# One product of 104 columns for y and the state in a chunked RWKV-7 kernel with a hard-swish feed-forward

## The chip, the cores and the metric

The kernel runs on one core of one Trainium2 chip. The metric is the device time of one execution in microseconds (us), as the median of several runs. Its engines are TensorE (PE; its weight loads are listed as PEld), VectorE (DVE), ScalarE (ACT), GpSimd (POOL) and SyncE, whose queue (SPq) issues nearly all DMAs.

## What is computed

Four sequences of 768 tokens, 8 heads of 40 features. A state of 40 x 40 per head is carried over the tokens; then comes a feed-forward with a hard-swish.

```python
for t in range(S):
    y[:, :, t] = np.einsum('bhd,bhde->bhe', rt, state)
    Sa = np.einsum('bhde,bhe->bhd', state, at)
    state_decay = state * wt[:, :, None, :] - np.einsum('bhd,bhe->bhde', Sa, bt)
    state = state_decay + np.einsum('bhd,bhe->bhde', vt, kt)
...
h = x @ w_in                       # x: y as (3072, 320); w_in: 320 x 2048
g = h * np.clip(h + 3.0, 0.0, 6.0) / 6.0
out = g @ w_out                    # w_out: 2048 x 320
```

All is fp32.

## The kernel before

**Units.** The recurrence is done in blocks of 64 tokens. A unit is such a block for two sequences, so a tile of 128 partitions holds 2 x 64 tokens (or 2 x 64 slots of features, 40 of them used). There are 24 units in 6 groups of 4. Unit i continues the state tile `state[i % 2]`.

**Stages ahead of the state** (`prepare`), which do not depend on it: W and gam (decays, by two scans on VectorE, lines 555 and 566), A, B and K (transposed a, b and k times decays), F (products of a and b; four units' F together are inverted by many small steps on VectorE and GpSimd, `invert`, into `tinv`), factor (decays turned, then k and b times them into `KBt`), E (masked scores of k and a) and EV (scores times v, line 701).

**Stages on the state** (`step`): RT and VT (turned r and v; the state is scaled by the decay, line 855), R and S (from the state), U and UT (by `tinv`, lines 906 and 926), rS (the part of y from the old state), C and H (scores, masked into one of three score buffers by `masked`, line 530; the scores' products are at line 522), sn (the new state: KBt's columns as weights, v and U as moving data, line 961; added at line 969), y (the same columns as weights, the masked scores as moving data, line 984; added at line 995 and multiplied by the decays on GpSimd at line 996), move and move2 (DMAs that bring y into the layout of the feed-forward, lines 1010 and 1015).

Most of these products are 64 x 64 or smaller and run as four independent ones on the quarters of the PE array. Each fp32 product leaves two records in the profile.

**Feed-forward** (`feed_forward`): products `h` (line 1066), relu and hard-swish into `gt` on ScalarE (1081) and VectorE (1082), products `o` (1107). `pieces` issues this work in small pieces between the blocks of the recurrence; two banks of `h` alternate, so the next products into a bank wait until its gt is done.

**Order.** All instructions are in a hand-written order on each engine's queue. From unit 4 on the loop goes by blocks, four to a unit. In each block `together` first issues the products of all stages that are due, by PRODUCTS, and then what follows them on the other engines, by RESULTS. It may use five PSUM banks at a time; where a stage would need more, it finishes what it has begun first. `ps_pair` places products of up to 512 columns in a pair of banks. Between blocks come pieces of feed-forward and steps of the inversion. In the steady state (units 8 and later) the stages of the current unit and those of the unit five ahead share the blocks:

| block | current unit | unit before | units ahead |
|---|---|---|---|
| 0 | RT, VT | y | W, gam; EV of the one before it |
| 1 | R, C, S | move, move2 | A, B |
| 2 | U, UT, rS | | F, K |
| 3 | sn, H | | E, factor |

Units 8 to 11 are prepared at a closer distance with CLOSE_STAGES.

Of the kernel before, what the change touches and what calls it, by code (L numbers as in the profile page):

```python
# [17 lines left out]
P = 128  # L18
# [13 lines left out]
def kernel(  # L32
# [178 lines left out]
    wms = [const.tile([P, SCAN + 1], F32, name=f"wm{i}") for i in range(2)]  # L211
    for t in wms:
        nc.vector.memset(t[:], 0.0)
# [6 lines left out]

    score = []
    for i in range(3):
        t = const.tile([P, H, BL], F32, name=f"score{i}")
        nc.gpsimd.memset(t[:], 0.0)
        score.append(t)
    turn = [0]

    values = [padded(const.tile([P, H, SLOT], F32, name=f"V{i}"), f"V{i}") for i in range(AHEAD)]
# [283 lines left out]
    def half(i, n=SLOT):  # L512
        return slice(SLOT * i, SLOT * i + n)

    def scores(lhs, rhs, swap=False):


        o = ps_pair(NPR, BL)
        for n in range(NPR):
            for q in range(2):  # L520
                for i in range(2):
                    nc.tensor.matmul(out=o[i][half(q), n, :],  # L522
                                     lhsT=lhs[half(i, D), n ^ (2 * q * swap), half(q)],
                                     rhs=rhs[half(i, D), n, half(q)], start=True, stop=True)
        return o

    def masked(o):
        turn[0] += 1
        x = score[turn[0] % len(score)]
        nc.vector.copy_predicated(out=x[:].rearrange("p (i h) t -> p i h t", i=2), mask=mask8, data=o[2])  # L530
        return x


    def prepare(i, F):
        n, o = i % NU, data[i]
        halves = i >= 2 * NU
        def w_stage():
            wt = turn_pairs(o["WN"])
            yield PE

            wm = o["wm"] = wms[i % 2]
# [12 lines left out]
            prods = o["prods"] = tmp.tile([P, NB, 2, HB + 1], F32, name="prods", bufs=2)  # L554
            nc.vector.tensor_tensor_scan(  # L555
                out=prods[:].rearrange("p r m i -> p (r m i)"), data0=wm[:, 0:SCAN], data1=start[:],
                initial=0.0, op0=ALU.mult, op1=ALU.add,
            )

        def gam_stage():  # L560

            prods, wm = o["prods"], o["wm"]
            first = start[:].rearrange("p (n i) -> p n i", i=HB + 1)[:, :, 0]
            nc.vector.reciprocal(first, prods[:].rearrange("p r m i -> p (r m) i")[:, ::-1, HB])
            back = _ap(wm[:], SCAN, [[-1, SCAN]])
            nc.vector.tensor_tensor_scan(out=back, data0=back, data1=start[:], initial=0.0,  # L566
                                         op0=ALU.mult, op1=ALU.add)
# [12 lines left out]

            copy(gv[:, :, 0:HB], _ap(o["wm"][:], HB + 1, [[row, NB], [-1, HB]]))
            copy(rv[:, :, HB:BL], _ap(o["wm"][:], HB + 3, [[row, NB], [1, HB]]))
            nc.gpsimd.tensor_copy(gv[:, :, HB:BL], o["prods"][:, :, 1, 0:HB])  # L583
            nc.gpsimd.tensor_copy(rv[:, :, 0:HB], o["prods"][:, :, 0, 0:HB][:, :, ::-1])
            dec = grp.tile([P, 2, 2, NPR], F32, name="dec", tag="dec", bufs=NU + 2)
            nc.gpsimd.tensor_copy(dec[:].rearrange("p m q r -> p r q m"),
                                  o["prods"][:].rearrange("p (r q) m i -> p r q m i", q=2)[:, :, :, :, HB])
            o["dec"] = dec
            if NU + 1 < i <= 2 * NU:
                fetch("V", i)  # L590
            yield from ()

        def a_stage():
            x = turn_in(o["AN"], halves)
            yield PE
            nc.vector.memset(_ap(o["wm"][:], 0, [[HB + 1, 2 * NB + 1]]), 0.0)
# [92 lines left out]
        def e_stage():  # L689
            x = scores(o["kt"], o["at"])  # L690
            yield PE
            o["E"] = masked(x)

        def ev_stage():

# [136 lines left out]
    def step(i):  # L832
# [52 lines left out]
        def s_S():  # L885
# [10 lines left out]
            new_U()  # L896
# [16 lines left out]
        def s_C():  # L913
            x = scores(m["VT"], m["RT"])
            yield PE
            m["K"] = masked(x)

        def s_UT():

            up = ps_pair(2, P)  # L920
# [11 lines left out]
            nc.scalar.activation(out=m["UT"][:].rearrange("p (x j) t -> p x j t", x=2), in_=up[2],  # L932
                                 func=AF.Copy, scale=-1.0)

        def s_rS():

# [12 lines left out]
                                 in_=ysp[2].rearrange("p r j q t -> p r j (q t)"), func=AF.Copy)  # L949

        def s_sn():
            wide = SLOT if i < NU else D
            sn = ps_pair(NPR, D)
            for name in "KB":
                for pr in range(NPR):
                    for s in range(2):
                        for q in range(2):
                            h = 2 * pr + s
                            by = VN[half(q), 4 * s + pr, 0:D] if name == "K" else \
                                m["U"][half(q), 4 * (s ^ q) + pr, 0:D]  # L960
                            nc.tensor.matmul(  # L961
                                out=sn[q][half(s, wide), pr, :],
                                lhsT=o[name][half(q), h * D:h * D + wide], rhs=by,
                                start=(name == "K" and pr == 0), stop=(name == "B" and pr == NPR - 1),
                            )
            yield PE
            for rows in [slice(0, P)] if i < NU else [half(s, D) for s in range(2)]:
                x = st[rows, :, :, 0:D]
                nc.vector.tensor_tensor(out=x, in0=sn[2][rows], in1=x, op=ALU.add)  # L969

        def s_H():
            x = scores(m["UT"], m["RT"], swap=True)
            yield PE
            m["B"] = masked(x)

        def s_y():
            y = ps_pair(NPR, BL)
# [35 lines left out]
        def s_move2():  # L1013
            for dst, src in m["moves"][4:]:
# [3 lines left out]

        return {"RT": s_RT, "R": s_R, "VT": s_VT, "S": s_S, "U": s_U, "C": s_C, "UT": s_UT,
                "rS": s_rS,  # L1020
                "sn": s_sn, "H": s_H, "y": s_y, "move": s_move, "move2": s_move2}

# [313 lines left out]
    for _ in range(18):  # L1336
# [149 lines left out]
```

## Time and profile before

| | |
|---|---|
| median of the runs shown | 788.37 us (788.35, 788.37, 791.86) |
| the profiled execution | 791.42 us, its span 789.7 us |
| mean granted TensorE clock | 0.963 |
| PE busy | 729.7 us (92%), 15832 instructions |
| DVE, ACT, POOL busy | 496.0, 320.6, 174.7 us |

The span is from the first to the last instruction. Busy times of PE overlap where products follow each other, since their ends are modelled; distances from start to start do not. Lines are those of the kernel before. A row of groups or of the timeline gives the line, the engine, the operation, the tiles written and read, and the shapes; in the timeline it begins with start and duration in us.

### The profile page before, as it was taken

What the parts mean: (1) busy time and instruction counts of PE and PEld (TensorE: products, weight loads), DVE (VectorE), ACT (ScalarE), POOL (GpSimd) and SP (SyncE); (2) the same over time, 40 slices, a digit from 0 to 9 for tenths busy, and PEclk for the clock granted to TensorE, in tenths of its full rate; (3) what the DMA queues carried; (4) which work ended last, traced back from release to release, by engine and by line L of the source; (5) the groups of instructions that cost most, each with busy time, mean ns of one, the idle gap of its engine ahead of it and who ended that gap; (6) DMA issues with size and microseconds to landing.
All of it is one profiled execution on the core that took longest, in us unless ns stands there. A gap on an engine that the chain in (4) does not pass through costs nothing.

```text
span 789.7 us, 35306 instructions
## 1 busy us (share of the span) xinstructions
PE 729.7 (92%) x15832; PEld 619.4 (78%) x15832; DVE 496.0 (63%) x971; ACT 320.6 (41%) x664; POOL 174.7 (22%) x318
## 2 busy tenths in 40 slices
PE   5726888999999989999999999999999999999998
PEld 4625777778778778888888888888888888888886
DVE  7899867699545699345988445987435982323210
ACT  2376865324445334444334444335434225412211
POOL 6403111322232304112404212304312202000000
PEclk9865699999999999999999999999999999999999
DMA  9684453311333313223213223213221101110000
GB/s 122 114 201 123 109 165 70 70 27 36 56 62 60 64 28 57 50 44 67 44 29 64 45 46 63 48 28 65 45 51 38 31 10 30 30 30 10 13 20 17
DMA packets 174215, 45.03 MB, mean 57 GB/s; under 512 B 157424, under 2 KB 172784, under 8 KB 174064
## 3 DMA queue, kind: packets, MB, share of 16 engines
q1 hardware_dynamic: 169760, 42.03, 27.5%
q8 instruction: 125, 2.05, 1.0%
q10 hardware_dynamic: 4304, 0.74, 0.7%
q14 instruction: 26, 0.21, 0.1%
HBM read 34.08 MB, written 3.93 MB: 48 GB/s over the span
## 4 chain that ended last, share of the span: by engine, by line
PE 80%; DVE 8%; DMA 4%; issue 3%; ACT 2%; SPq 2%; POOL 0%; DVEq 0%
PE h L1066 27%; PE o L1107 24%; PE pair L522 4%; PE pair L984 3%; PE one L484 2%; PE pair L494 2%; PE pair L961 2%; PE pair L906 2%; PE pair L868 1%; PE pair L926 1%; PE pair L942 1%; SPq L468 1%; PE pair L811 1%; PE pair L701 1%; DVE wm L566 1%
## 5 line engine op out<-in xcount | busy, mean ns | idle before, releaser
L1066 PE MATMUL h<-xt,win 128*128 128x128 f32 (+1 forms) x2304 | 249.0, 282 | 3.3 <-DVE gt L1082 3.3
L1066 PEld LDWEIGHTS h<-xt,win 128*128 128x128 f32 (+1 forms) x2304 | 229.6, 191 | 20.3 <-issue 4.2
L1107 PE MATMUL o<-wout,gt 128*128 128x320 f32 x768 | 229.6, 442 | 0.0
L1107 PEld LDWEIGHTS o<-wout,gt 128*128 128x128 f32 x768 | 138.1, 190 | 50.2
L1082 DVE SCALAR_TENSOR_TENSOR gt<-gt,h 128x512 f32<-128x512 f32 x96 | 62.0, 681 | 74.4 <-ACT gt L1081 74.4
L1081 ACT ACTIVATE gt<-h,three 128x512 f32<-128x512 f32 x96 | 62.1, 686 | 96.0 <-PE h L1066 95.6
L996 POOL TENSOR_TENSOR yg<-ys,gam 128x512 f32<-128x512 f32 x22 | 39.0, 1772 | 156.7 <-DVE ys L995 77.1
L753 DVE TENSOR_TENSOR prod<-x 128x30 f32<-128x30 f32 (+9 forms) x180 | 67.2, 373 | 8.9 <-POOL x L738 3.3
L674 POOL TENSOR_TENSOR KBt<-K,rgt 128x320 f32<-128x320 f32 x22 | 19.0, 865 | 217.8 <-ACT rgt L663 169.6
L759 DVE TENSOR_TENSOR x<-x,prod 128x30 f32<-128x30 f32 (+9 forms) x180 | 62.2, 346 | 5.5
L969 DVE TENSOR_TENSOR state<-pair,state 40x320 f32<-40x320 f32 (+1 forms) x43 | 21.0, 488 | 62.8 <-PE pair L961 36.5
L530 DVE COPY_PREDICATED score<-mask,pair 128x512 f32<-128x512 int32 x72 | 50.6, 722 | 1.5 <-PE pair L522 1.0
L995 DVE TENSOR_TENSOR ys<-pair,ys 128x512 f32<-128x512 f32 x22 | 15.2, 690 | 40.5 <-PE pair L701 21.5
L566 DVE TENSOR_TENSOR_SCAN wm<-wm,start 128x528 f32<-128x528 f32 x24 | 37.7, 1571 | 0.8
L555 DVE TENSOR_TENSOR_SCAN prods<-wm,start 128x528 f32<-128x528 f32 x24 | 30.0, 1252 | 9.2 <-ACT wm L551 9.1
L846 ACT ACTIVATE RT<-pair 128x512 f32<-128x512 f32 x22 | 13.1, 597 | 54.2 <-PE pair L494 52.5
L706 ACT ACTIVATE EV<-pair 64x320 f32<-64x320 f32 x44 | 19.0, 432 | 33.1 <-PE pair L701 22.3
L821 ACT ACTIVATE tinv<-pair 32x256 f32<-32x256 f32 x48 | 18.0, 375 | 33.9 <-PE pair L811 33.3
L1125 ACT ACTIVATE ob<-o 128x320 f32<-128x320 f32 x22 | 9.6, 435 | 50.3 <-PE o L1107 26.0
L583 POOL COPY gam<-prods 128x256 f32<-128x256 f32 x24 | 22.0, 917 | 33.3 <-DVE prods L555 32.5
L984 PE MATMUL pair<-score,KBt 64*64 64x64 f32 x1408 | 26.1, 221 | 1.7 <-DVE score L530 1.4
L872 DVE TENSOR_TENSOR RR<-pair,EV 128x320 f32<-128x320 f32 x22 | 10.7, 486 | 26.0 <-PE pair L522 26.0
(272 smaller groups left out, 1078.4 us busy)
## 6 DMA issues: line engine op xcount, KB each, us to landing
V<-in_v_dram SPq DMA_DIRECT2D x96, 40.0 KB
out_dram<-ob SPq DMA_DIRECT2D x47, 80.0 KB
R<-in_r_dram SPq DMA_DIRECT2D x92, 40.0 KB
B<-in_b_dram SPq DMA_DIRECT2D x42, 80.0 KB
K<-in_k_dram SPq DMA_DIRECT2D x42, 80.0 KB
W<-in_w_dram SPq DMA_DIRECT2D x37, 80.0 KB
A<-in_a_dram SPq DMA_DIRECT2D x37, 80.0 KB
xt<-yg SPq DMA_DIRECT2D x72, 40.0 KB
```

Of the source, the lines that this page charges most:

```text
L522: nc.tensor.matmul(out=o[i][half(q), n, :], lhsT=lhs[half(i, D), n ^ (2 * q * swap), half(q)], rhs=rhs[half(i, D), n, half(q)], start=True ...
L530: nc.vector.copy_predicated(out=x[:].rearrange("p (i h) t -> p i h t", i=2), mask=mask8, data=o[2])
L555: nc.vector.tensor_tensor_scan(out=prods[:].rearrange("p r m i -> p (r m i)"), data0=wm[:, 0:SCAN], data1=start[:], initial=0.0, op0=ALU.m ...
L566: nc.vector.tensor_tensor_scan(out=back, data0=back, data1=start[:], initial=0.0, op0=ALU.mult, op1=ALU.add)
L753: nc.vector.tensor_tensor(out=pv, in0=_ap(x[:], (i + 1) * L + i, [[L, n], [0, i]]), in1=_ap(x[:], i * L, [[0, n], [1, i]]), op=ALU.mult,)
L759: nc.vector.tensor_tensor(out=rest, in0=rest, in1=pv, op=ALU.add)
L984: nc.tensor.matmul(out=y[q][half(s), pr, :], lhsT=o[name][half(q), h * D:h * D + SLOT], rhs=m[name][half(q), 4 * rs + 2 * s + j, :], start ...
L996: nc.gpsimd.tensor_tensor(out=yg[:], in0=m["ys"][:].rearrange("p r q t -> p r (q t)"), in1=o["G"][:], op=ALU.mult)
L1066: nc.tensor.matmul(out=hp[c][:, i, :], lhsT=lhsT, rhs=rhs, start=(begun[c] == 0), stop=(begun[c] == 3 * NQ - 1))
L1081: nc.scalar.activation(out=gt[:], in_=hp[c][:], func=AF.Relu, bias=three[:], scale=1.0)
L1082: nc.vector.scalar_tensor_tensor(out=gt[:], in0=gt[:], scalar=6.0, in1=hp[c][:], op0=ALU.min, op1=ALU.mult)
L1107: nc.tensor.matmul(out=op[:], lhsT=gts[c][:, n, :], rhs=wout[:, c * HJ + r * NQ + n, :], start=((split or r == 0) and c == 0 and n == 0), ...
```

## The change

From unit 4 on sn and y become one stage, ysn. Its moving data are 104 columns: 64 of masked scores and, behind them, 40 of v (with k's columns as weights) or of U (with b's). For that the score buffers of these units are two tiles of 8 x 104 columns, `beside`; ScalarE writes U straight behind the scores, GpSimd copies v there in stage C. H's scores and U are placed so that both have the same order of heads. U and UT share one pair of banks in a new arrangement. The weights are 64 columns wide; the state is added over 128 partitions at once. E of the units ahead has a buffer of its own, and EV moves to block 3 of the next unit ahead (three empty stages before it in AHEAD_STAGES). The second buffer of the decays (`wms`) and the score buffers lie in one tile `area`, whose space the new tiles take over; from unit 8 on one decay buffer is left.

```diff
+    EDGE = 2 * (SCAN + 1)
+    area = const.tile([P, EDGE + 3 * H * BL], F32, name="area")
+    wms = [area[:, i * (SCAN + 1):(i + 1) * (SCAN + 1)] for i in range(2)]
...
-    def scores(lhs, rhs, swap=False):
+    def scores(lhs, rhs, swap=False, placed=False):
...
-                    nc.tensor.matmul(out=o[i][half(q), n, :],
+                    nc.tensor.matmul(out=o[i][half(q), n ^ (2 * q * placed), :],
...
+    JOIN = BL + D
+    beside = {}
+    def begun_beside():
+        begin = -(-(SCAN + 1) // 16) * 16
+        for n, name in enumerate("KB"):
+            x = area[:, begin + n * H * JOIN:begin + (n + 1) * H * JOIN]
+            nc.gpsimd.memset(x, 0.0)
+            beside[name] = x.rearrange("p (h t) -> p h t", h=H)
+        beside["E"] = grp.tile([P, H, BL], F32, name="E", tag="U", bufs=1)
+        nc.gpsimd.memset(beside["E"][:], 0.0)
...
-            wm = o["wm"] = wms[i % 2]
+            wm = o["wm"] = wms[i % 2 if i < 2 * NU else 0]
...
-            o["E"] = masked(x)
+            o["E"] = masked(x, beside.get("E") if halves else None)
...
+            if i >= NU:
+                up = m["up"] = ps_pair(512)
+                for pr in range(NPR):
+                    at = pr // 2 * 256 + pr % 2 * D
+                    for s in range(2):
+                        for x in range(2):
+                            nc.tensor.matmul(out=up[x][half(x ^ s), at:at + D],
+                                             lhsT=tinv[half(x), n * H + 4 * s + pr, :],
+                                             rhs=m["R"][half(x), s, pr, :], start=True, stop=True)
+                yield PE
+                nc.scalar.activation(out=_ap(beside["B"], BL, [[JOIN, 4], [4 * JOIN, 2], [1, D]]),
+                                     in_=_ap(up[2], 0, [[256, 4], [D, 2], [1, D]]), func=AF.Copy, scale=-1.0)
+                return
...
+            m["K"] = masked(x, beside["K"][:, :, 0:BL])
+            nc.gpsimd.tensor_copy(beside["K"][:, :, BL:JOIN].rearrange("p (r x) d -> p r x d", r=2),
+                                  VN[:].rearrange("p (x r) d -> p r x d", r=2)[:, :, :, 0:D])
...
-            m["B"] = masked(x)
+            m["B"] = masked(x, None if i < NU else beside["B"][:, :, 0:BL])
+        def s_ysn():
+            both = ps_pair(NPR, JOIN)
+            for name in "KB":
+                for pr in range(NPR):
+                    j, rs = pr // 2, pr % 2
+                    for s in range(2):
+                        for q in range(2):
+                            h = 2 * pr + s
+                            nc.tensor.matmul(
+                                out=both[q][half(s), pr, :], lhsT=o[name][half(q), h * D:h * D + SLOT],
+                                rhs=beside[name][half(q), 4 * rs + 2 * (s ^ (q * (name == "B"))) + j, :],
+                                start=(name == "K" and pr == 0), stop=(name == "B" and pr == NPR - 1))
+            yield PE
+            yg = m["yg"] = tmp.tile([P, NPR, P], F32, name="yg", tag="yg", bufs=2)
+            x = m["ys"][:].rearrange("p r q t -> p q r t")
+            nc.vector.tensor_tensor(out=x, in0=both[2][:, :, :, 0:BL], in1=x, op=ALU.add)
+            nc.gpsimd.tensor_tensor(out=yg[:], in0=m["ys"][:].rearrange("p r q t -> p r (q t)"),
+                                    in1=o["G"][:], op=ALU.mult)
+            x = st[:, :, :, 0:D]
+            nc.vector.tensor_tensor(out=x, in0=both[2][:, :, :, BL:JOIN], in1=x, op=ALU.add)
...
-    OWN_STAGES = [["RT", "VT"], ["R", "C", "S"], ["U", "UT", "rS"], ["sn", "H"], ["y"],
+    OWN_STAGES = [["RT", "VT"], ["R", "C", "S"], ["U", "UT", "rS"], ["H"], ["ysn"],
                   ["move", "move2"]]
-    AHEAD_STAGES = [["W", "gam"], ["A", "B"], ["F", "K"], ["E", "factor"], ["EV"]]
+    AHEAD_STAGES = [["W", "gam"], ["A", "B"], ["F", "K"], ["E", "factor"], [], [], [],
+                    ["EV"]]
...
-                "y", "EV", "R", "C", "U", "UT", "rS", "sn", "H", "E", "F"]
+                "ysn", "EV", "R", "C", "U", "UT", "rS", "H", "E", "F"]
-    RESULTS = ["RT", "y", "W", "VT", "EV", "R", "S", "C", "A", "B", "move", "move2",
-               "U", "UT", "rS", "F", "K", "sn", "H", "E", "factor", "gam"]
+    RESULTS = ["RT", "ysn", "W", "VT", "EV", "R", "S", "C", "A", "B", "move", "move2",
+               "U", "UT", "rS", "F", "K", "H", "E", "factor", "gam"]
...
-    WIDTH = {"R": NPR * D, "U": NPR * D, "sn": NPR * D, "EV": NPR * D}
+    WIDTH = {"R": NPR * D, "U": 512, "UT": 0, "ysn": NPR * JOIN, "EV": NPR * D}
...
     m = 0
+    begun_beside()
     for i in range(NU, NK):
```

Units 0 to 3 keep sn and y.

More of the change, by code (lines that the diff above doesn't have):

```diff
@@ L210 @@
     nc.vector.memset(start[:].rearrange("p (n i) -> p n i", i=HB + 1)[:, :, 0:1], 1.0)
-    wms = [const.tile([P, SCAN + 1], F32, name=f"wm{i}") for i in range(2)]
+    EDGE = 2 * (SCAN + 1)
+    area = const.tile([P, EDGE + 3 * H * BL], F32, name="area")
+    wms = [area[:, i * (SCAN + 1):(i + 1) * (SCAN + 1)] for i in range(2)]
     for t in wms:
-        nc.vector.memset(t[:], 0.0)
+        nc.vector.memset(t, 0.0)
     inputs, others = {}, {}
@@ L222 @@
     for i in range(3):
-        t = const.tile([P, H, BL], F32, name=f"score{i}")
-        nc.gpsimd.memset(t[:], 0.0)
-        score.append(t)
+        t = area[:, EDGE + i * H * BL:EDGE + (i + 1) * H * BL]
+        nc.gpsimd.memset(t, 0.0)
+        score.append(t.rearrange("p (h t) -> p h t", h=H))
     turn = [0]
@@ L525, in scores, with masked @@
         return o
-    def masked(o):
-        turn[0] += 1
-        x = score[turn[0] % len(score)]
+    JOIN = BL + D
[8 more added lines that the diff above has]
+        nc.gpsimd.memset(beside["E"][:], 0.0)
+    def masked(o, x=None):
+        if x is None:
+            turn[0] += 1
+            x = score[turn[0] % len(score)]
         nc.vector.copy_predicated(out=x[:].rearrange("p (i h) t -> p i h t", i=2), mask=mask8, data=o[2])
@@ L564, in gam_stage @@
             nc.vector.reciprocal(first, prods[:].rearrange("p r m i -> p (r m) i")[:, ::-1, HB])
-            back = _ap(wm[:], SCAN, [[-1, SCAN]])
+            back = _ap(wm, SCAN, [[-1, SCAN]])
             nc.vector.tensor_tensor_scan(out=back, data0=back, data1=start[:], initial=0.0,
@@ L579, in copy @@
                     nc.vector.tensor_scalar(to, x, 1.0, None, ALU.mult)
-            copy(gv[:, :, 0:HB], _ap(o["wm"][:], HB + 1, [[row, NB], [-1, HB]]))
-            copy(rv[:, :, HB:BL], _ap(o["wm"][:], HB + 3, [[row, NB], [1, HB]]))
+            copy(gv[:, :, 0:HB], _ap(o["wm"], HB + 1, [[row, NB], [-1, HB]]))
+            copy(rv[:, :, HB:BL], _ap(o["wm"], HB + 3, [[row, NB], [1, HB]]))
             nc.gpsimd.tensor_copy(gv[:, :, HB:BL], o["prods"][:, :, 1, 0:HB])
@@ L595, in a_stage @@
             yield PE
-            nc.vector.memset(_ap(o["wm"][:], 0, [[HB + 1, 2 * NB + 1]]), 0.0)
+            nc.vector.memset(_ap(o["wm"], 0, [[HB + 1, 2 * NB + 1]]), 0.0)
             at = o["at"] = grp.tile([P, NPR, P], F32, name="at", tag="at")
@@ L895, in s_S @@
             nc.scalar.activation(out=S[:], in_=sp[:], func=AF.Copy)
-            new_U()
+            if i < NU:
+                new_U()
         def s_U():
@@ L915, in s_C @@
             yield PE
-            m["K"] = masked(x)
+            if i < NU:
+                m["K"] = masked(x)
+                return
+            m["K"] = masked(x, beside["K"][:, :, 0:BL])
+            nc.gpsimd.tensor_copy(beside["K"][:, :, BL:JOIN].rearrange("p (r x) d -> p r x d", r=2),
+                                  VN[:].rearrange("p (x r) d -> p r x d", r=2)[:, :, :, 0:D])
         def s_UT():
-            up = ps_pair(2, P)
+            late = i >= NU
+            up = m["up"] if late else ps_pair(2, P)
+            if late:
+                up = [_ap(x, 2 * D, [[256, 2], [1, P]]) for x in up[:2]] + [_ap(up[2], 2 * D, [[256, 4], [1, P]])]
             for j in range(2):
@@ L931, in s_UT @@
             m["UT"] = turned("UT")
-            nc.scalar.activation(out=m["UT"][:].rearrange("p (x j) t -> p x j t", x=2), in_=up[2],
-                                 func=AF.Copy, scale=-1.0)
+            nc.scalar.activation(out=m["UT"][:] if late else m["UT"][:].rearrange("p (x j) t -> p x j t", x=2),
+                                 in_=up[2], func=AF.Copy, scale=-1.0)
         def s_rS():
@@ L951, in s_sn @@
         def s_sn():
-            wide = SLOT if i < NU else D
             sn = ps_pair(NPR, D)
@@ L961, in s_sn @@
                             nc.tensor.matmul(
-                                out=sn[q][half(s, wide), pr, :],
-                                lhsT=o[name][half(q), h * D:h * D + wide], rhs=by,
+                                out=sn[q][half(s), pr, :],
+                                lhsT=o[name][half(q), h * D:h * D + SLOT], rhs=by,
                                 start=(name == "K" and pr == 0), stop=(name == "B" and pr == NPR - 1),
@@ L966, in s_sn @@
             yield PE
-            for rows in [slice(0, P)] if i < NU else [half(s, D) for s in range(2)]:
-                x = st[rows, :, :, 0:D]
-                nc.vector.tensor_tensor(out=x, in0=sn[2][rows], in1=x, op=ALU.add)
+            x = st[:, :, :, 0:D]
+            nc.vector.tensor_tensor(out=x, in0=sn[2], in1=x, op=ALU.add)
         def s_H():
-            x = scores(m["UT"], m["RT"], swap=True)
+            x = scores(m["UT"], m["RT"], swap=True, placed=i >= NU)
             yield PE
-            m["B"] = masked(x)
+            m["B"] = masked(x, None if i < NU else beside["B"][:, :, 0:BL])
[17 more added lines that the diff above has]
+                                    in1=o["G"][:], op=ALU.mult)
+            x = st[:, :, :, 0:D]
+            nc.vector.tensor_tensor(out=x, in0=both[2][:, :, :, BL:JOIN], in1=x, op=ALU.add)
         def s_y():
@@ L1020, in step @@
                 "rS": s_rS,
-                "sn": s_sn, "H": s_H, "y": s_y, "move": s_move, "move2": s_move2}
+                "sn": s_sn, "ysn": s_ysn, "H": s_H, "y": s_y, "move": s_move, "move2": s_move2}
     HJ, NQ = NJ // 2, 4
```

## The prediction

> **What bounds the kernel now.** I read the page first: the span, the slices by engine, the chain that ended last.
>
> ```profile
> span 789.7 us, 35306 instructions
> ...
> PE   5726888999999989999999999999999999999998
> ...
> PE 80%; DVE 8%; DMA 4%; issue 3%; ACT 2%; SPq 2%; POOL 0%; DVEq 0%
> ```
>
> From the sixth slice on TensorE is nearly always busy, and 80% of the chain runs through it. The loop that the change touches (units 4 to 23) starts at about 190 us and ends at 749 us; in the windows 300 to 750 TensorE is busy 49.2 to 50.0 us of every 50. So what the change takes off TensorE's queue there comes off the end nearly whole, and what it takes off VectorE counts only where TensorE waits for VectorE. VectorE is close to full at the inversions (43.45 us of 500 to 550).
>
> Next the timeline of TensorE in a steady unit, first block 3, then block 0 of the next unit:
>
> ```profile
> 442.19 0.41 PE L654 MATMUL pair<-ident,rgam 64*128 64x64 f32 x8
> 442.52 0.52 PE L961 MATMUL pair<-V,KBt 64*40 64x40 f32 x32
> 442.85 0.55 PE L961 MATMUL pair<-U,KBt 64*40 64x40 f32 x32
> 443.23 0.69 PE L522 MATMUL pair<-RT,UT 40*64 40x64 f32 x32
> 443.72 0.68 PE L522 MATMUL pair<-at,kt 40*64 40x64 f32 x32
> ...
> 448.65 1.16 PE L984 MATMUL pair<-score,KBt 64*64 64x64 f32 x64
> 449.63 0.63 PE L701 MATMUL pair<-V,score 64*64 64x40 f32 x32
> 450.19 0.54 PE L1107 MATMUL o<-wout,gt 128*128 128x320 f32 x1
> ```
>
> What counts is start to next start (busy times overlap). The state's sums (line 961) take 442.52 to 443.23, 0.71 us; y's (984) 448.65 to 449.63, 0.98 us; scores times v of the unit ahead (701) 0.56 us. Each fp32 product is two records, and four run at once on quarters of the array, so each 64 records are 16 sets of four.
>
> **The price of a set.** From the starts of single records in the trace, one set follows another (weight columns/moving columns) after: 40/40 (line 961) 38.3 ns; 64/40 (line 868, and unit 3's line 961, whose weights are 64 wide) 58.2; 64/64 (984) 58.2; on the whole array 128/128 (1066) 111.7 and 128/320 (1107) 269.4. That is 0.833 ns a column of the longer side, plus 5 ns where the weights are as long or longer and 2.7 where the moving side is. So the state's sets are cheap because their weights are 40 wide, and a y set is already as long as its 64 columns: little is paid twice now. With 64/104 the moving side sets the pace: 86.7 + 2.7 to 5 = 89.4 to 91.7 ns, 16 sets 1.43 to 1.47 us. No group of four in this trace has a longer moving than weight side; unhidden loads (53.3 ns more) would make a set 145 ns, no overhead at all 86.7. I take 89.4, as in the only row with a longer moving side.
>
> [...]
>
> **Part by part.**
>
> Block 0: y and line 701 were 0.98 + 0.56 = 1.54 us. Now one group: 1.43 us of sets, the 0.05 of entering that y shows (0.98 less 16 x 58.2 ns) and the 0.09 of changing to the feed-forward products that 701 shows (0.56 less 8 x 58.2): 1.57, so +0.03 (+0.07 at 91.7 ns). Block 3: the 0.71 of line 961 goes; 701 comes, 8 x 58.2 = 0.47 and 0.02 to 0.05 for entering: 0.49, so -0.22 (-0.19). Per unit -0.19 us (from -0.12), over 20 units **-3.8 us** (from -2.4).
>
> VectorE: in block 3 two additions go, and in block 0 one comes, ahead of the unit ahead's decay scans:
>
> ```profile
> L969 DVE TENSOR_TENSOR state<-pair,state x43: 474/493/500, 73.0 to 742.0; 40x320 f32<-40x320 f32 x40, 128x320 f32<-128x320 f32 x3
> ```
> ```profile
> 505.70 0.69 DVE ys L995
> 506.39 1.18 DVE prods L555
> ...
> 507.88 1.85 DVE wm L566
> ...
> 510.49 0.60 DVE gt L1082
> ...
> 511.23 1.13 PE h L1066 x8
> ```
>
> The first line is from the view of the state's addition: 0.49 us, whether over 40 rows or 128. The others are the chain of waits, in order of time. There TensorE does wait, 0.20 us, for the feed-forward's gt, which stands behind both scans on VectorE. y's addition used to wait for line 701, which shares its banks (1.68 us after y's first product); now it waits for a group of 1.48 us and some 0.25 of latency, 1.73, and then the state's addition delays the scans 0.49 more: gt comes 0.54 us later. I paired each gt with the first product that needs its bank free. In the loop the margin is under 0.2 us at 244.0, 274.8, 394.8 and 511.2 us, and 2.3 us or more everywhere else. The last three follow the scans directly, 3 x 0.54: **+1.6 us**. If a wait further down hides one, 0.5 less; the place at 244 comes 9 us after its scan and I count none there.
>
> Banks: a block may hold five. U with UT now fills a pair of banks alone, so in unit 4's block 2 the products of rS and F come after a first round of results instead of F alone; rS waits for ScalarE's copy of unit 8's decays (0.44 us), and in block 0 of unit 5 line 701 has a round of its own. Together **+0.4 us**, once; between 0, since ysn's 1.5 us covers the copies, and 1.3, the longest such wait now (line 634, 1.2 us).
>
> Waits that go: y's groups in the loop take 20.96 us against 20 x 0.98 = 19.6, so 1.3 us is waiting. The masked scores that they wait for come 1 us earlier, since no state addition (0.99 us) stands ahead of them on VectorE in block 3. I take half, **-0.6 us** (from 0 to -1.3).
>
> GpSimd: one copy of v per unit, 128x320. The nearest rows are 0.40 to 1.25 us for the 128x256 copies (line 583), so 0.5 to 1.6; it is issued in block 1 and read three blocks later, behind the 0.25 us memset of U that goes. GpSimd idles 15 us at a stretch in that part of the unit (470.90 line of the timeline), so nothing; were that cover gone, the block's yg would come up to 1.6 us later. The zeroing at the loop's start is 2176 columns, 2.2 us by the 0.524 us of line 224 for 512, ahead of unit 4's scale; the state is needed 2 us after that by TensorE (195.5 us), so 0 to 0.5, nothing taken. ScalarE's copies are as many and as long; those of line 701 move to block 3, in place of rgt's waiting for the state's addition (35.8 us in total, 12 times). The queue of loads keeps its order; v's next load no longer waits for line 961, which was not late. At the end y's longer group delays its transposed moves by 0.45 us, but the 6.1 us of feed-forward that cover them start as much later: nothing. A single decay buffer and a single E have whole blocks between their uses: nothing.
>
> Sum: -3.8 + 1.6 + 0.4 - 0.6 = -2.4 us. It is made against the profiled execution, 791.42 us (its span 789.7 and 1.7 around it), which is 3.05 above the median of 788.37; two runs of the three are at 788.35 and 788.37. Nothing in the sum depends on that, so I set it against the median: **786.0 us**, 0.3% faster.
>
> **Rivals.**
>
> *More comes back* (782.4). The waits of TensorE on ScalarE and VectorE in the loop add up to some 6 us; block 3 has half a microsecond net less of VectorE and no ScalarE wait for it. If half of these (3 us) go and the scans' delay is absorbed by what VectorE no longer does before: -3.8 - 3 + 0.8 = -6.0. For it: the 35.8 us of rgt's waits. Against: these waits are ScalarE's, and TensorE shows almost none behind them.
>
> *A fixed price a set* (779.6). If the state's sets, where they follow others, held the array as long as a set of 64 columns, dropping 16 would free 16 x 58.2 = 0.93 us a unit instead of 16 x 38.3 = 0.61: 6.4 us more over 20 units. For: 64/40 costs as much as 64/64. Against: the 0.71 us from the group's start to the next start has no room for 0.93. [...]
>
> *The wide set does not hide its loads* (slower). Place: the new group; price: 145 instead of 89.4 ns, 16 x 55.6 = 0.89 us a unit, 17.8 in all less 2.4: 803.8. It cancels the forecast's gain above 89.4 + 2.4/320 = 97 ns a set, and decides (over 0.5% slower) from 109 ns. For: no such group in the trace. Against: 128/320 hides loads that are 106.7 ns by the same law.
>
> *VectorE's lateness spreads* (slower). If the 0.54 us were paid in every block 0, it would cost 20 x 0.54 = 10.8 instead of 1.6: 795.2. It decides from 15 blocks of 20. Against: margins of 2.3 us elsewhere.
>
> That the change does not do what it says is excluded by the code: the two old groups load the same columns, 40 of them for the state and 64 for y.
>
> **How the numbers follow.** Forecast 0.55. Its own range is 783.5 to 788.9: downwards one delay hidden, banks at 0, all 1.3 of waiting gone and sets at 86.7 ns (0.9 more), -4.9; upwards 91.7 ns and full entry costs, no waiting gone and banks at 1.3, +0.5. More comes back 0.25, a fixed price 0.04; unhidden loads 0.09; spreading 0.07. About 0.5% (3.9 us) is what a measurement here can tell from no change. Faster by more: 0.25 + 0.04 and 0.09 of the forecast, 0.38. Slower by more: 0.09 + 0.07 = 0.16. Within: the forecast's other 0.46. The range, 780.5 to 790.5, takes the forecast, the first rival and the beginning of spreading; it leaves out up to 0.2.
>
> **What would show it.** Sets of the new group 89 to 92 ns apart, its start to the next start 1.5 to 1.6 us; line 701 in block 3 at 0.5; 1280 records fewer; gt waits of about 0.7 us at the three places. Sets over 97 ns, or such waits at other places, would make the forecast wrong upwards; shorter waits of TensorE throughout, downwards.

## The result, and the profile after

| | before | after |
|---|---|---|
| median of 19 runs each | 790.93 us (788.35 to 793.60) | 786.44 us (783.66 to 788.48) |
| profiled execution | 791.42 us, span 789.7 | 785.40 us, span 783.7 |
| ratio of the runs, 95% interval | | 0.9941 (0.9928 to 0.9954) |

The change makes the kernel 0.59% faster, 4.5 us by the medians and 6.0 between the two profiled executions. Executions of one kernel spread over 5 us, and in the traces of this study the first product of unit 4 stands anywhere between 188.3 and 194.0 us. So below **the loop** is compared: the records of the products h are counted off in 48 groups of 48 (half units of feed-forward), and the loop runs from the first record of the seventh group to the first of the 48th (185.3 to 772.2 us before). It lasts 586.9 us before and 581.6 after, **-5.3 us**; a second trace of the kernel before has 587.8.

The page of the kernel after; its span, slices and chain answer to those of before, and the group is the joint product:

```profile
span 783.7 us, 32780 instructions
...
PE   5636788999999989999999999999999999999998
...
PE 77%; DVE 10%; issue 6%; DMA 2%; ACT 2%; POOL 2%; SPq 1%; POOLq 0%; ACTq 0%; DVEq 0%
...
L1021 PE MATMUL pair<-area,KBt 64*64 64x104 f32 x1280 | 33.1, 252 | 0.0
```

TensorE still sets the pace; 1280 products' records are gone (15832 to 14552). The timeline of TensorE after, in the unit that was shown of before (block 3, then block 0):

```profile
438.41 0.41 PE L670 MATMUL pair<-ident,rgam 64*128 64x64 f32 x8
438.75 0.68 PE L717 MATMUL pair<-V,E 64*64 64x40 f32 x32
439.23 0.67 PE L524 MATMUL pair<-RT,UT 40*64 40x64 f32 x32
...
444.63 1.66 PE L1021 MATMUL pair<-area,KBt 64*64 64x104 f32 x64
446.22 1.07 PE L1165 MATMUL o<-wout,gt 128*128 128x320 f32 x3
```

From start to next start the joint product takes 1.59 us where y and scores times v took 1.54, and in block 3 scores times v takes 0.48 where the state's sums took 0.71. The chain of waits at the place that the prediction showed of 506 to 511 us:

```profile
499.08 1.63 PE pair L1021 x64
...
500.74 0.69 DVE ys L1028
501.43 0.40 DVE state L1032
501.83 2.08 DVE prods L571
...
504.22 1.32 DVE area L582
...
506.10 0.61 DVE gt L1140
506.70 0.14 issue
506.84 1.13 PE h L1124 x8
```

The state's addition (0.40 us of the chain) now stands ahead of the two scans, y's addition starts 1.73 us after the joint product's first record (499.01), and TensorE waits 0.77 us for gt where it waited 0.20. All waits of the products h for gt in the loop, before and after (total us, number, longest):

```profile
PE h L1066 <- DVE gt L1082: 0.6, 3, 0.2
```
```profile
PE h L1124 <- DVE gt L1140: 1.9, 3, 0.8
```

By place they are 0.23, 0.20 and 0.20 us before and 0.31, 0.77 and 0.77 after, 1.2 more in all.

So these two steps came much as forecast. Over the 20 units the groups of lines 961, 984 and 701 take 43.7 us from start to next start before, 0.4 of it a hole of the kind shown below, and those of 1021 and 717 take 39.9 after: -3.4 us. With the 1.2 of waiting that makes -2.2 of the -5.3. Most of the rest lay in rows that the prediction had passed over. In the timeline of TensorE before:

```profile
451.46 0.25 PE L788 MATMUL pair<-tb,F 32*32 32x32 f32 x5
452.11 0.71 PE L788 MATMUL pair<-tb,F 32*32 32x32 f32 x59 [0.40 <-issue]
```

and after:

```profile
447.49 0.75 PE L804 MATMUL pair<-tb,F 32*32 32x32 f32 x64
```

Before, 64 records of one group are split after the fifth by 0.59 us (start to start) in which TensorE waits for no engine ("issue"). There are five such holes in the loop before, of 0.46, 0.75, 0.59, 0.50 and 0.80 us, 3.1 together (each with a usual distance of some 0.04 in it); after there is one, 0.24. They go with a queue on the page, that of instructions:

```profile
q8 instruction: 125, 2.05, 1.0%
```
```profile
q8 instruction: 115, 1.88, 1.0%
```

These are loads of 16 KB (125 before, 115 after). TensorE has 31981 instructions in the trace before and 29437 after, semaphore instructions among them: 124.9 and 115.0 times 256, so one load to 256 instructions. Counted off by 256, every hole lies at the 193rd; and each ends 1.27 to 1.50 us after a load has landed, whether it is 0.24 or 0.80 us long.

The boundaries without a hole say the same. Counted through all 13 traces of this study, TensorE's instructions stand in order of their starts, a boundary lies behind the 193rd of each 256, and the second boundary is paired with the first load, the third with the second and so on. In all 1542 pairs the first instruction behind a boundary starts 1.17 us or more after its load has landed, while the last one ahead of it can start up to 1.45 us before that landing. So at these places TensorE went on no earlier than 1.17 us after the landing, and the loads cost nothing where it got there later than that anyway.

### The profile page after: what moved, and what is told of

Its sections match the earlier page's. It is cut to its first block, busy times and chain, and to the rows that moved or that the text cites. A ratio compares the mean times of both kernels' runs of the same rounds, so it can differ in the third digit from the quotient of the medians.

```text
span 783.7 us, 32780 instructions
## 1 busy us (share of the span) xinstructions
PE 725.0 (93%) x14552; PEld 613.3 (78%) x14552; DVE 486.6 (62%) x951; ACT 320.2 (41%) x664; POOL 171.9 (22%) x321
## 4 chain that ended last, share of the span: by engine, by line
PE 77%; DVE 10%; issue 6%; DMA 2%; ACT 2%; POOL 2%; SPq 1%; POOLq 0%; ACTq 0%; DVEq 0%
PE h L1124 27%; PE o L1165 25%; PE pair L1021 4%; PE pair L524 4%; PE pair L496 2%; PE one L486 2%; DVE prods L571 2%; PE pair L884 2%; PE pair L925 1%; PE pair L717 1%; DVE prod L769 1%; PE pair L964 1%; DVE x L775 1%; PE pair L980 1%; PE one L906 1%
## 5 line engine op out<-in xcount | busy, mean ns | idle before, releaser
L546 DVE COPY_PREDICATED area<-mask,pair 128x512 f32<-128x512 int32 x56 | 40.4, 724 | 62.2 <-PE pair L524 52.8
L769 DVE TENSOR_TENSOR prod<-x 128x30 f32<-128x30 f32 (+9 forms) x180 | 65.5, 364 | 8.9 <-POOL x L754 3.3
L775 DVE TENSOR_TENSOR x<-x,prod 128x30 f32<-128x30 f32 (+9 forms) x180 | 64.3, 357 | 5.5
L1029 POOL TENSOR_TENSOR yg<-ys,gam 128x512 f32<-128x512 f32 x20 | 25.4, 1272 | 126.1 <-DVE ys L1028 83.2
L690 POOL TENSOR_TENSOR KBt<-K,rgt 128x320 f32<-128x320 f32 x22 | 19.1, 870 | 151.4 <-ACT rgt L679 139.9
L571 DVE TENSOR_TENSOR_SCAN prods<-area,start 128x528 f32<-128x528 f32 x24 | 40.8, 1703 | 9.7 <-ACT area L567 9.6
L1021 PE MATMUL pair<-area,KBt 64*64 64x104 f32 x1280 | 33.1, 252 | 0.0
L582 DVE TENSOR_TENSOR_SCAN area<-area,start 128x528 f32<-128x528 f32 x24 | 31.1, 1297 | 0.8
L1021 PEld LDWEIGHTS pair<-area,KBt 64*64 64x64 f32 x1280 | 29.1, 133 | 1.4
L950 POOL COPY area<-V 128x320 f32<-128x320 f32 x20 | 9.1, 455 | 84.6 <-DVE area L612 52.9
L600 POOL COPY rgam<-prods 128x256 f32<-128x256 f32 x22 | 24.9, 1131 | 0.0
```

What stands on the lines that cost most here:

```text
L571: nc.vector.tensor_tensor_scan(out=prods[:].rearrange("p r m i -> p (r m i)"), data0=wm[:, 0:SCAN], data1=start[:], initial=0.0, op0=ALU.m ...
L769: nc.vector.tensor_tensor(out=pv, in0=_ap(x[:], (i + 1) * L + i, [[L, n], [0, i]]), in1=_ap(x[:], i * L, [[0, n], [1, i]]), op=ALU.mult,)
L775: nc.vector.tensor_tensor(out=rest, in0=rest, in1=pv, op=ALU.add)
L1021: nc.tensor.matmul(out=both[q][half(s), pr, :], lhsT=o[name][half(q), h * D:h * D + SLOT], rhs=beside[name][half(q), 4 * rs + 2 * (s ^ (q ...
L1029: nc.gpsimd.tensor_tensor(out=yg[:], in0=m["ys"][:].rearrange("p r q t -> p r (q t)"), in1=o["G"][:], op=ALU.mult)
```

## The experiments

Theory 1: what the prediction counted (shorter sets, gt later at three places), and beside it fewer holes, because dense small products outran the loading of instructions before and the joint product does not. Rivals: chance (holes lie elsewhere in another execution), position (the boundaries of the loads happened to lie well after the change), the moved stage, or sets whose price the sum had wrong. Sums of holes are those of the loop.

**The kernel before once more.**

> The kernel before once more, unchanged, for a second trace of it. In the first trace five groups of small products (blocks at 240.6, 326.7, 451.5, 531.7 and 568.7 us) have a hole of 0.46 to 0.80 us in their middle, where TensorE waits for no other engine; each hole begins 0.6 to 0.9 us after a 16 KB load of instructions has landed. The trace of the changed kernel has one such hole, of 0.24 us. Theory 1 (the holes belong to the order of the program: dense small products run ahead of the loading of instructions): the same places again, some 3 us in all in the loop. Theory 2 (chance): other places, or a sum that differs by more than 1 us.

792.43 us in its one run. Holes of 0.45, 0.48, 1.02 and 1.46 us, 3.4 together, at 241.0, 327.2, 531.4 and 569.0 us: four of the five places; the one at 451 us is missing. So the places belong to the program, the lengths to the execution.

**The joint product cut in two, weights of 64 columns.**

```diff
-            for name in "KB":
+            for name, cols in [(x, y) for x in "KB" for y in (slice(0, BL), slice(BL, JOIN))]:
+                wide = SLOT if cols.start == 0 else SLOT
...
-                                out=both[q][half(s), pr, :], lhsT=o[name][half(q), h * D:h * D + SLOT],
-                                rhs=beside[name][half(q), 4 * rs + 2 * (s ^ (q * (name == "B"))) + j, :],
-                                start=(name == "K" and pr == 0), stop=(name == "B" and pr == NPR - 1))
+                                out=both[q][half(s, wide), pr, cols], lhsT=o[name][half(q), h * D:h * D + wide],
+                                rhs=beside[name][half(q), 4 * rs + 2 * (s ^ (q * (name == "B"))) + j, cols],
+                                start=(name == "K" and pr == 0 and cols.start == 0),
+                                stop=(name == "B" and pr == NPR - 1 and cols.start > 0))
```

> The changed kernel with its product of 104 columns cut into one of 64 and one of 40 again, both with weights of 64 columns, in the same block, banks and buffers. Theory 1 (a set of four goes at the pace of its longer side, 0.833 ns a column and 3 to 5 ns): 16 x (58.2 + 58.2 - 89.4) = 0.43 us more a unit, 8.6 us over 20 units, so 795.0 us, 1.005 of the kernel before; and holes in the middle of groups come back, up to 3 us more, if they come from the density of records. Theory 2 (a set costs its columns, whatever its weights: 64 and 40 cost 58.2 and 38.3): 16 x (58.2 + 38.3 - 89.4) = 0.11 us more a unit, 2.3 us in all, 788.7 us, 0.997.

798.18 us, 1.0108 (1.0082 to 1.0133). The loop is 594.9 us, 13.4 more than after. The product's groups take 43.6 instead of 31.6 us; without the 2.7 us of four holes inside them this is 9.2 more, where 8.6 was expected. Holes in all: 5.3 us at nine places. Theory 1 in both its parts, with more holes than it allowed for: the expected 1.005 counted none, and up to 3 us were named beside it.

**The same with weights of 40 columns for the state's part**, that is, only the joining undone. The lines that differ from the run above:

```diff
-                wide = SLOT if cols.start == 0 else SLOT
+                wide = SLOT if cols.start == 0 else D
...
-            x = st[:, :, :, 0:D]
-            nc.vector.tensor_tensor(out=x, in0=both[2][:, :, :, BL:JOIN], in1=x, op=ALU.add)
+            for rows in [half(s, D) for s in range(2)]:
+                x = st[rows, :, :, 0:D]
+                nc.vector.tensor_tensor(out=x, in0=both[2][rows, :, :, BL:JOIN], in1=x, op=ALU.add)
```

> The changed kernel with its product of 104 columns cut into one of 64 columns (weights 64 wide) and one of 40 (weights 40 wide), as in the kernel before, but in one block, with the new buffers and the new place of scores times v; the state is added in two halves of 40 rows. Only the joining is undone. Sets: 16 x (58.2 + 38.3 - 89.4) = 0.11 us and one more group to enter, 0.05: 0.16 us a unit, 3.3 us in all; the second addition on VectorE delays gt at three places, 1.5 us. Theory 1 (holes in the middle of groups come with the density of records): 2.5 to 3 us of holes come back, 794 us, 1.004 of the kernel before. Theory 2 (the holes belonged to the old order of blocks): none come back, 791.2 us, 1.0003.

794.32 us, 1.0053 (1.0036 to 1.0070), the loop 590.0 us. A steady group lasts 1.73 us instead of 1.59, so 2.8 us in the loop where 3.3 were expected. Holes: 5.8 us at ten places, five of them inside the cut product. The timeline of TensorE in one of them:

```profile
238.80 1.13 PE L1022 MATMUL pair<-area,KBt 64*40 64x40 f32 x75
240.73 0.28 PE L1022 MATMUL pair<-area,KBt 64*40 64x40 f32 x6 [0.80 <-issue]
```

The 2.8 of sets and the 5.6 of additional holes (5.8 less 0.24) are the 8.4 us by which the loop is longer than that of the changed kernel. Theory 1, with more holes than expected again. With its new order and buffers but without the joining the kernel is slower than before: what the change gives, the joining gives.

**Wider weights in the kernel before.**

```diff
-            wide = SLOT if i < NU else D
+            wide = SLOT
...
-            for rows in [slice(0, P)] if i < NU else [half(s, D) for s in range(2)]:
+            for rows in [slice(0, P)]:
```

> The kernel before with weights of 64 instead of 40 columns in the state's sums from unit 4 on (as many records; the state added over 128 rows in one instruction). Theory 1 (a set goes at the pace of its longer side): its sets take 58.2 instead of 38.3 ns, 0.32 us a unit, 6.4 us in all, 1.008; with fewer records a microsecond the holes behind these groups (326.7 and 531.7 us, 1.3 us together) shrink, then 1.0065. Theory 2 (a set costs its moving columns): no change, 1.000.

793.66 us, 1.0049 (1.0033 to 1.0066). The state's sums take 19.1 instead of 13.6 us in the loop (0.27 us a unit where 0.32 was expected): weights of 64 columns set the pace of these products of 40. The loop grows by only 3.5 us, mainly since holes fall from 3.1 to 1.6 us; another 0.5 was not traced. As many records, but slower ones, had fewer holes here.

**Scores times v back in block 0.**

```diff
-    AHEAD_STAGES = [["W", "gam"], ["A", "B"], ["F", "K"], ["E", "factor"], [], [], [],
+    AHEAD_STAGES = [["W", "gam"], ["A", "B"], ["F", "K"], ["E", "factor"],
                     ["EV"]]
```

> The changed kernel with scores times v of the units ahead back in block 0, where it was before. It no longer fits the pair of banks of the joint product (416 + 160 columns), so that it comes in a round of its own. Theory 1 (it has to wait for ScalarE's copies of RT and VT out of the banks, some 2.2 us against the 1.5 us of the joint product): 0.5 to 0.7 us in 12 units, 6 to 8 us more than the changed kernel, 793 us, 1.003 of the kernel before. Theory 2 (the joint product hides those copies): 0.05 us a unit, 787 us, 0.995.

790.69 us, 1.0009 (0.9998 to 1.0020), the loop 587.1 us, 5.5 more than after. Its waits of TensorE:

```profile
PE pair L717 <- ACT VT L895: 4.5, 12, 0.9
```

12 waits for ScalarE to clear VT's banks, 0.4 us each, a little less than the 0.5 to 0.7 expected. So the other half of the change, the new place, is needed to keep what the joining gives. Holes: 0.3 us, so it is not the new place that removes them.

**The boundaries moved by half a load**, in the kernel before and after: 64 products of 32x32 ahead of everything.

```diff
+    shift = bank("one", [P, 512], 1)
+    for n in range(64):
+        nc.tensor.transpose(out=shift[0:L, 0:L], in_=ident[0:L, 0:L], identity=ident[0:L, 0:L])
```

> The kernel before with 64 products of 32x32 ahead of everything on TensorE (128 instructions, in the 12 us in which TensorE waits for the first loads; their result is read by nobody), so that all later instructions lie half a 16 KB load further on. In all traces so far each hole in the middle of a group lies at the 192nd or 193rd of every 256 instructions of TensorE (16 KB) and ends 1.2 to 1.6 us after such a load has landed. Theory 1 (a load's boundary inside small products that follow each other densely stops TensorE; density decides how much): the five holes are gone from their places, others stand at the new boundaries, 2 to 4 us in all in the loop, ratio to the kernel before 1.000. Theory 2 (position alone decides, and this kernel had bad luck): under 1 us, ratio 0.996 to 0.998.

> The changed kernel with the same 64 products ahead of everything. Theory 1 (the joint product's 64 records take 1.43 us instead of 0.93 and scores times v has left their block, so that a load is seldom outrun): at most 1.5 us of holes, ratio to the kernel before 0.994 to 0.996. Theory 2 (the changed kernel had good luck with its boundaries): 2 to 4 us of holes, ratio 0.997 to 0.999.

Before, moved: 793.05 us, 1.0029 (1.0013 to 1.0044), a little more than the 1.000 expected; its loop, 587.7 us, is that of the second trace of the kernel before (587.8). Its holes lie at other groups, the longest now among the state's sums:

```profile
326.17 0.51 PE L961 MATMUL pair<-U,KBt 64*40 64x40 f32 x31
327.89 0.23 PE L961 MATMUL pair<-U,KBt 64*40 64x40 f32 x1 [1.21 <-issue]
```

They come to 3.0 us, at the 192nd or 193rd of 256 instructions again. After, moved: 787.44 us, 0.9961 (0.9941 to 0.9981), one hole of 0.8 us, the loop 582.2 us. Both as theory 1 has it: boundaries choose the places, density the sum. The gap between the two moved kernels is 5.5 us of loop (587.7 and 582.2), that of the unmoved 5.3.

**The state's addition last in its block.**

```diff
+            m["both"] = both
+
+        def s_st():
             x = st[:, :, :, 0:D]
-            nc.vector.tensor_tensor(out=x, in0=both[2][:, :, :, BL:JOIN], in1=x, op=ALU.add)
+            nc.vector.tensor_tensor(out=x, in0=m["both"][2][:, :, :, BL:JOIN], in1=x, op=ALU.add)
+            yield from ()
...
-               "U", "UT", "rS", "F", "K", "H", "E", "factor", "gam"]
+               "U", "UT", "rS", "F", "K", "H", "E", "factor", "gam", "st"]
```

> The changed kernel with the addition of the state moved behind the decay scans, their copies and all other results of its block on VectorE. Theory 1 (the addition ahead of the scans delays gt at three places, where the trace of the changed kernel loses 0.57, 0.62 and 0.62 us): the waits of the products h for gt fall from 1.9 to some 0.6 us, the loop is 1.4 us shorter, ratio to the kernel before 0.9923. Theory 2 (VectorE is full there anyway, and what is late next takes the place): waits for gt or for the masked scores stay, ratio 0.994.

794.47 us, 1.0053 (1.0034 to 1.0072): slower, which neither theory had. The longest waits of TensorE in its loop:

```profile
PE pair L884 <- DVE state L1035: 4.0, 3, 1.3
PE pair L496 <- DVE state L1035: 2.3, 2, 1.2
...
PE h L1128 <- DVE gt L1144: 1.2, 2, 0.6
```

The edit misses its aim. In its timeline the addition (391.05 us) still stands ahead of gt (391.45), behind the scans instead of before them, so gt gains little: the two longest waits for it are 0.59 instead of 0.77 us. And the next block's products (lines 496 and 884) wait for the addition, 6.3 us in five waits, the longest 1.3. Those of line 496 turn inputs and read no state, so what they wait for (2.3 us of the 6.3) is the joint product's banks, which stay occupied until the addition is done. The loop is 591.2 us; the waits for the addition explain 6.3 of its 9.6 us over the changed kernel, holes 1.0 more, and the rest was not traced.

**W's results ahead of the joint product's.**

```diff
-    RESULTS = ["RT", "ysn", "W", "VT", "EV", "R", "S", "C", "A", "B", "move", "move2",
+    RESULTS = ["RT", "W", "ysn", "VT", "EV", "R", "S", "C", "A", "B", "move", "move2",
```

> The changed kernel with the results of W (copies on ScalarE, first scan on VectorE) issued ahead of those of the joint product, so that VectorE scans while TensorE still sums. Theory 1 (gt stands behind y's addition, the state's addition and both scans; 1.25 us of that chain now lies beside the product): no wait of h for gt is left, loop 1.9 us shorter, ratio 0.992. Theory 2 (y's addition becomes late instead: its product on GpSimd and the moves come 0.5 to 1 us later, and the feed-forward waits for them): ratio 0.994 or more, with waits of h for the moves.

784.22 us, 0.9929 (0.9909 to 0.9950). No wait of h for gt over 0.15 us is left in the loop, which lasts 579.8 us, 1.8 less than after (1.9 expected); holes 0.2 us. Theory 1. The times alone would not separate it from the changed kernel, their intervals overlap; the loops do.

**Stages of the transition moved as well**: factor and scores times v of unit 8 and scores times v of unit 11, each one block later, on top of the edit above.

```diff
+    EXTRA = {2 * NU: [["W", "gam"], ["A", "B"], ["F", "K"], ["E", "factor"], [], ["EV"]],
+             3 * NU - 1: [["W", "gam"], ["A", "B"], ["F", "K", "factor"], ["E"], [], ["EV"]]}
...
-            ahead[u, m] = prepared(u), CLOSE_STAGES if close else AHEAD_STAGES
+            ahead[u, m] = prepared(u), EXTRA.get(u) or (CLOSE_STAGES if close else AHEAD_STAGES)
```

> The changed kernel with the results of W ahead of those of the joint product (as in the run w_first), and two stages of the transition elsewhere: factor of unit 8 one block later and its scores times v one block later, scores times v of unit 11 one block later. In the trace of w_first TensorE waits there 1.1 us for UT's copy (line 980), 0.5 and 1.5 us ahead of scores times v (line 717). Theory 1 (these are waits for banks, gone where the stage has room): 3 us less than w_first, some 781.5 us, 0.988. Theory 2 (the next stage waits for the same copies): within 1 us of w_first, 0.992.

> The kernel of w_first_places with the same 64 products ahead of everything. Its trace has 2.4 us of holes (two of 0.85 and 0.94 us in F's products at 546 and 572 us), w_first's 0.2. Theory 1: the boundaries leave these two groups, holes under 1.5 us in all, 781.5 us, ratio 0.9885. Theory 2 (the holes come from this order of stages, not from the boundaries): 2 us or more stay at the same groups, 0.9907.

782.73 us, 0.9907 (0.9891 to 0.9922): the lowest median, 1.5 us under the run with W's results first where 3 were expected, so between the two theories; their intervals overlap. The waits of 1.1 and 1.5 us are gone, that of 0.5 stays, but holes rose to 2.4 us, since its boundaries fall into F's products. The loop does not confirm the gain: it lasts 580.8 us, 1.0 more than with W's results first (1.1 less without the holes of both), and what the traced execution is faster by lies ahead of the loop, which begins at 183.0 instead of 185.1 us.

Moved by half a load the holes fall to 0.9 us at another group, as theory 1 expected, and the loop is 580.0 us. Yet the whole takes 786.17 us, 0.9943 (0.9922 to 0.9965), where 781.5 were expected. In its trace unit 4 begins at 194.0 us instead of 188.3, but that execution (787.89 us) is the longest of the seven; what happens ahead of the loop there was not followed up. So the last two runs show where the holes go, not what moving these stages is worth.

## Why the prediction was right, and where not

The time, 786.0 forecast and 786.44 measured, agrees better than the reasoning, and that is luck: the forecast was a gain of 2.4 us against 788.37, but the kernel before is at 790.93 over 19 runs, 2.6 higher, and the gain is 2.1 us larger. The two errors cancel. The direction, the place and the price of the new group were right by reasoning. The gain is 4.5 us, 0.59%, so just outside the band in which the forecast's case mostly lay, on the side that the rival "more comes back" stood for, though not by its mechanism: what came back were not waits for ScalarE and VectorE.

*The price of a set*: taken 89.4 ns, measured 89.4. The joint group lasts 1.59 us (1.57 forecast), scores times v in block 3 0.48 (0.49): -0.18 us in a steady unit where -0.19 was taken. In seven of the 20 units no scores times v stood behind y, so that the sum over the loop is -3.4 where -3.8 was taken. The runs with cut products and with wide weights say the same of the law behind it. The rival of unhidden loads (145 ns) is out; that of a fixed price too, as a 64/40 group cut off cost 0.46 us a unit (9.2/20) and a 40/40 one 0.14.

*gt later at three places*: 0.54 us each forecast, 1.6 in all. At two places the wait grew by 0.57 us, at the first by 0.08 only, 1.2 in all: there no scores times v stood behind y, the joint product is 0.50 us longer than y's group was (1.59 and 1.09), and TensorE itself comes later. (The lead of the kernel after falls by 0.57, 0.62 and 0.62 us at the three places, which the expectation of the run with the state's addition last takes for lost in waiting; it holds what the joint product is longer by.) Of the sign that the prediction named, waits of about 0.7 us, two of three came. The fourth narrow place, counted at none, showed no loss. Lateness did not spread: no other wait of h for gt appeared.

*Banks*, +0.4: the round of unit 4's block 2 waits 1.1 us for UT's copy, but F no longer waits 1.2 us; unit 8's scores times v waits 0.4 us less than before. The sum is about -0.5: mis-sized by 0.9, because the waits that the new rounds replace were counted at nothing.

*Waits that go*, -0.6: the reading was wrong. Of the 1.3 us by which y's groups exceeded 20 x 0.98, 0.4 was a hole. Most of the rest is 0.11 us in each of the seven groups behind which feed-forward products follow instead of scores times v (1.09 against 0.98 us), the price of changing to these. In the loop no record of line 984 waits for the masked scores, so there was nothing for their coming earlier to save.

*What failed*: the sum had no term for instruction loads. It took the distances within dense groups as constant and "issue" as small change, where five rows of the timeline were split in their middle. Its own mechanism was right, and about 2.9 us more came back (3.1 less 0.24). Together: -3.4 + 1.2 - 0.5 - 2.9 = -5.6 against the -5.3 of the loop; the other 0.3 us were not taken apart.

Why density matters can only be estimated. By the ends of all holes a load is of use 1.2 to 1.6 us after it has landed, and the loads of the loop take 0.9 to 1.6 us before that, 2.1 to 3.2 us together. 128 records with their weight loads are 256 instructions: at 64/64 they last 1.9 us (32 sets of 58.2 ns), at 64/104 2.9. So if a load is asked for no more than 256 instructions ahead, the first would outrun it where a whole one lies in dense work, and the second seldom. When a load is asked for was not found out.

## What to carry to other kernels

Joining two products that share their weights saved little in the sets themselves here, which already went at the pace of their columns (2.8 us of a loop of 590.0 by the run with weights of 40 columns). The sets of four here cost what their longer side did, weights or moving data (38.3 ns at 40/40, 58.2 at 64/40 and 64/64, 89.4 at 64/104): price a set so, and ask whether the shorter product was bound by it at all. Then look at the distances inside dense groups of small products too: a group split in its middle with "issue" beside it may be waiting for its own instructions. Here its place in the count of instructions (the 193rd of 256) and the landing of a load (1.27 to 1.50 us before the end of the hole) showed it, and with fewer, longer products 0.24 of 3.1 us was left. An addition put ahead of a long chain on another engine was paid by TensorE where it waited for the end of that chain (0.57 us at two places here); placing the chain's first step beside the product took that back (the loop fell by 1.8 us).

## What the runs showed of the hardware that was not expected

- TensorE stopped for 0.2 to 1.5 us at the 192nd or 193rd of every 256 of its instructions when small products ran densely there. All these holes, in every trace, ended 1.2 to 1.6 us after a 16 KB load of instructions landed, and no boundary was passed earlier than 1.17 us after the landing of its load. Sums in the loop: 3.0 to 3.4 us in three traces of the kernel before, moved or not; 1.6 with slower sets; 5.3 and 5.8 with the joint product cut; 0.2 to 0.9 in five of the traces with it whole, 1.2 and 2.4 in the two others.
- 64 more products (128 instructions) at the start of the kernel before moved all its holes to other groups (3.0 us in all, the longest with 1.21 us of idle time in line 961).
- In groups of four on quarters of the array, weights of 64 columns hold a set of 40 moving columns to 58.2 ns (38.3 with weights of 40), and in the kernel before with wider weights the state's sums grew from 13.6 to 19.1 us by it. With 64 weight columns and 104 moving ones a set took 89.4 ns.
